# Unordered indirect writes and a different split of rounding work in an attention, mixture-of-experts and dense kernel

## The chip, the cores and the metric

The kernel runs on one core of a Trainium2 chip. The metric is the device time of one execution in microseconds (us); three runs of the kernel before are shown, and one further execution was profiled. A difference of under 1% is about what cannot be told from no change here.

## The reference

Three layers follow each other: attention whose queries are averaged in pairs, a mixture of eight experts of which each token takes one, and a dense layer with a squared ReLU. All data is float32.

```python
q_pool = q.reshape(B, H, S // 2, 2, D).mean(axis=3)
attn = softmax(q_pool @ k.T / sqrt(D))
x = (attn @ v) as (2304, 512)                  # B*S = 2304 tokens
expert_idx = argmax(normalized(x) @ normalized(emb).T / tau)
for e in range(8):                             # one expert for each token
    h = maximum(x[mask] @ w1[e], 0)            # 512 -> 1024
    out[mask] = gate_w[mask] * (h @ w2[e])     # 1024 -> 512
h = out @ w_in                                 # 512 -> 2048
g = maximum(h, 0) ** 2
result = g @ w_out                             # 2048 -> 512
```

## The kernel before

**Numbers as two halves.** TensorE multiplies 16-bit values. A float32 operand is kept as a high half (the value rounded by ScalarE, `hi`) and a low half (the value minus `hi`, by GpSimd or VectorE, `lo`), and each product is three matmuls: hi·hi, hi·lo, lo·hi. `w_in` and `w_out` lie in HBM as 64-bit numbers; `split64` first makes a float32 out of each pair of words with three VectorE operations (L1156, L1161, L1165), and then rounds it with ScalarE (L1170) and GpSimd (L1172). Such a unit of 128x512 is a *piece* here; each of the two matrices has 16 of them.

**Stages.** Attention and routing fill the first 500 us. The expert stage (some 500 to 757 us) goes over tiles of T = 192 rows sorted by expert. `tile_a(t)` multiplies by w1, ReLU goes to ScalarE (`hh`, L1281) and its low half to VectorE (`hl`, L1282), and `tile_b(t)` multiplies by w2. When the expert changes, `splits` makes the halves of the next expert's weights (`ws`): high halves by ScalarE and VectorE, low halves by VectorE and, for some, GpSimd (L1248). Into tiles 3 to 15 other work is dealt out: pieces of `w_in`, whose loads (`win_load`, L1149) GpSimd issues into two buffers of the tile `fill`; and, two for each of the tiles 3 to 11, the calls of `send`: an indirect DMA (L1132), also issued by GpSimd, that writes the gate and the row number of 128 tokens to their places in the HBM table `cm`. The rows are taken from `ci`, so that the program cannot know which rows of `cm` one write touches. SyncE loads weights (L1206) and transposed tokens (`x`, L1212).

**Dense layer.** `Ffn.run` takes the 2304 tokens in six blocks of 384. `first(tt)` computes 16 column groups `f` of the hidden layer (L1446, 12 matmuls each, called a *step* here); block 0 has its first 8 done in the expert stage (F1 = 8), so that `first(0)`, `first(1)`, `first(2)` are 40 steps, one after the other, before the first `second(tt)`. After a step's matmuls ScalarE takes the ReLU (L1451, `r`), VectorE squares it (L1452), and one step later `halves` makes `gh` by ScalarE (L1465) and `gl` by GpSimd (L1466). The steps' PSUM tiles come from two pools, chosen by `f % 5`: three buffers in `ps_b` and two in `ps_a`; `f` starts again at 0 in each block, so that f = 15, 0, 1, 2 follow each other in `ps_b`. During these 40 steps the generator `convert` also turns `w_out` into halves: after each step three parts of it are recorded.

**Order.** Every engine runs its instructions in the order in which this code records them. An engine waits on semaphores for data of others and for buffers to come free; the recording layer adds a wait for every earlier access to the same bytes.

Of the kernel before, what the change touches and what calls it, by code (L numbers as in the profile page):

```python
# [12 lines left out]
U32 = mybir.dt.uint32  # L13
ACTF = mybir.ActivationFunctionType
ALU = mybir.AluOpType
# [798 lines left out]
class Moe:  # L814
# [301 lines left out]
    def places(self, small):  # L1116

        nc = self.nc
        V = nc.vector
        d = small.tile([128, E], F32, tag="d", name="d")  # L1120
        V.tensor_tensor(out=d, in0=self.off[:, 1], in1=self.c("ecap"), op=ALU.subtract)
        pr = small.tile([128, 18, E], F32, tag="sq", name="prd")
        V.tensor_tensor(
            out=pr, in0=self.oh, in1=d[:, None, :].to_broadcast([128, 18, E]), op=ALU.mult
        )
        cp = small.tile([128, 18], F32, tag="cp", name="cp")
        V.tensor_reduce(out=cp, in_=pr, axis=AX.X, op=ALU.add)
        ci = small.tile([128, 18], I32, tag="ci", name="ci")
        V.tensor_tensor(out=ci, in0=cp, in1=self.rix, op=ALU.add)

        def send(n):
            nc.gpsimd.indirect_dma_start(  # L1132
                out=self.cm[:, :], out_offset=bass.IndirectOffsetOnAxis(ap=ci[:, n:n + 1], axis=0),
                in_=self.meta[:, n], in_offset=None, bounds_check=NTOK - 1,
            )

        return send

# [267 lines left out]
class Ffn:  # L1406
# [29 lines left out]
            self.hidden(0, f, ps, self.tmp[f % 2], self.g0[:, 0, f], self.g0[:, 1, f])  # L1436
            self.done += 1

    def hidden(self, tt, f, ps, r, gh, gl):
        nc = self.nc  # L1440
        c0 = slice(tt * self.N, tt * self.N + self.N)
        fs = slice(128 * f, 128 * f + 128)
        m = 0
        for k in range(4):
            for wh, yh in ((0, 0), (0, 1), (1, 0)):
                nc.tensor.matmul(  # L1446
                    out=ps, lhsT=half(self.win[wh][:, k, fs], wh), rhs=self.yT[yh][:, k, c0],
                    start=(m == 0), stop=(m == 11),
                )
                m += 1  # L1450
        nc.scalar.activation(out=r, in_=ps, func=ACTF.Relu)  # L1451
        nc.vector.scalar_tensor_tensor(  # L1452
            out=r, in0=ps, scalar=0.0, in1=r, op0=ALU.max, op1=ALU.mult
        )
        self.pend.append((r, gh, gl))
        if len(self.pend) > 1:
            self.halves()

# [2 lines left out]
            self.halves()  # L1461

    def halves(self):
        g, hi, lo = self.pend.pop(0)
        self.nc.scalar.activation(out=hi, in_=g, func=ACTF.Copy)  # L1465
        self.nc.gpsimd.tensor_tensor(out=lo, in0=g, in1=hi, op=ALU.subtract)  # L1466

    def run(self, ctx):
        nc, moe, N = self.nc, self.moe, self.N
        pool = lambda n, b, **kw: ctx.enter_context(moe.tc.tile_pool(name=n, bufs=b, **kw))  # L1470
        stg = pool("stg2", 2)
# [11 lines left out]
        so = {}  # L1483

        def wout_load(n):
            so[n] = stg.tile([128, 1024], U32, tag="g64", name="g64")
            moe.load64(so[n], moe.w_out[128 * n:128 * n + 128, :], nc.sync)

        def convert():
            for n in range(16):  # L1490
                f = stg.tile([128, 512], U32, tag="f32", name="f32")
                split = moe.split64(so.pop(n), f, wout[0][:, n], wout[1][:, n])
                for i, _ in enumerate(split):
                    yield
                    if i == 2:
                        yield
                if n + 2 < 16:
                    wout_load(n + 2)
                yield

        wout_load(0)
        wout_load(1)
# [5 lines left out]
        def first(tt):  # L1508
            g = G[tt] = {}
            for f in range(0 if tt else F1, 16):  # L1510
# [2 lines left out]
                gh, gl = [a[:, f % 8] for a in g[f // 8]]  # L1513
                ps = (ps_a if f % 5 in (3, 4) else ps_b).tile([128, N], F32, tag="a", name="a")
                r = rp.tile([128, N], F32, tag="r", name="r")
                self.hidden(tt, f, ps, r, gh, gl)
                if tt < 3:
                    for _ in range(3):
                        next(conv, None)
            self.finish()  # L1520

# [353 lines left out]
```

## Time and profile before

| | us |
|---|---|
| three runs | 1138.07, 1147.18, 1143.66 |
| median | 1143.66 |
| profiled execution, its own time | 1142.18 |
| span of its trace | 1140.4 |
| TensorE (PE) busy | 1061.1 (93%) |
| VectorE (DVE) busy | 722.1 (63%) |
| GpSimd (POOL) busy | 531.3 (47%) |
| ScalarE (ACT) busy | 527.5 (46%) |

TensorE is busy for nearly all of the span, so the rest of the reading is about the places where it is not, and about those where its granted clock is low. Times below count from the span's start.

### The profile page before, as it was taken

How to read it: one execution, taken by the hardware profiler on the slowest of the kernel's cores; microseconds unless marked ns; L12 is line 12 of the kernel's file. 1: busy time of each engine (PE TensorE's matmuls, PEld its weight loads, DVE VectorE, ACT ScalarE, POOL GpSimd, SP SyncE). 2: the span in 40 equal slices, each digit the busy share in tenths (PEclk: the TensorE clock that was granted, in tenths of full speed). 3: DMA queues.
4: the chain of work that ended last, by engine and by line, in shares of the span. 5: the costliest groups of instructions: out<-in, count | busy, mean ns of one | idle time of the engine just before them, and what ended most of it. 6: DMA issues, size and time to landing. Idle time of an engine off the chain costs nothing. (4 is left out here: it accounts for less than half of the span.)

```text
span 1140.4 us, 28256 instructions
## 1 busy us (share of the span) xinstructions
PE 1061.1 (93%) x11340; PEld 724.6 (64%) x11340; DVE 722.1 (63%) x1374; ACT 527.5 (46%) x998; POOL 531.3 (47%) x454
## 2 busy tenths in 40 slices
PE   6898899999999889999899799998799999999996
PEld 2465556656665566999899699975454454555543
DVE  6999989999998988866664548848850021211200
ACT  5776677678876756423222335534440031322200
POOL 4765655566765646522443426637760142322301
PEclk9999989999998989999999899999899999999998
DMA  8665765656766537569579699223310000000000
GB/s 221 146 141 155 192 160 123 145 141 143 155 135 139 110 67 194 142 190 226 103 96 231 140 228 272 55 52 104 108 38 19 29 10 20 10 10 20 10 19 28
DMA packets 170830, 128.98 MB, mean 113 GB/s; under 512 B 129816, under 2 KB 134040, under 8 KB 170672
## 3 DMA queue, kind: packets, MB, share of 16 engines
q1 hardware_dynamic: 164912, 109.09, 41.8%
q0 software_dynamic: 5760, 17.85, 5.2%
q8 instruction: 91, 1.49, 0.6%
q14 instruction: 67, 0.55, 0.2%
HBM read 74.69 MB, written 12.60 MB: 77 GB/s over the span
## 5 line engine op out<-in xcount | busy, mean ns | idle before, releaser
L425 POOL TENSOR_TENSOR pl<-p 128x512 f16<-128x512 f32 x144 | 176.8, 1233 | 155.1 <-ACT p L415 150.1
L415 ACT ACTIVATE p<-st 128x512 f32<-128x512 f32 x288 | 169.4, 598 | 81.1 <-PE st L397 78.2
L397 PE MATMUL st<-r,t 128*128 128x64 f16 (+3 forms) x1152 | 198.8, 294 | 8.3 <-ACT p L415 7.7
L1446 PE MATMUL a<-yT,win 128*128 128x384 f16 x1056 | 178.6, 333 | 11.3 <-DVE r L1452 8.8
L462 PEld LDWEIGHTS <-p 128*128 128x128 bf16 x2304 | 135.9, 99 | 59.6 <-issue 6.7
L1446 PEld LDWEIGHTS <-win 128*128 128x128 f16 (+1 forms) x1152 | 114.4, 99 | 89.7 <-issue 18.7
L462 PE MATMUL pv<-vx,p 128*128 128x65 f16 x2250 | 159.9, 197 | 2.4 <-DVE xb L503 2.4
L1531 PE MATMUL o<-wo,gh 128*128 128x512 f16 (+1 forms) x528 | 157.0, 379 | 0.0
L462 PE MATMUL pv<-vx,pl 128*128 128x65 f16 x1125 | 144.7, 194 | 0.0
L425 DVE TENSOR_TENSOR pl<-p 128x512 f16<-128x512 f32 x144 | 141.5, 984 | 3.5 <-ACT p L415 3.5
L1451 ACT ACTIVATE r<-a 128x384 f32<-128x384 f32 x88 | 42.6, 486 | 185.6 <-PE a L1446 138.6
L1398 PEld LDWEIGHTS <-ws 128*128 128x128 f16 (+1 forms) x1344 | 114.0, 100 | 15.7 <-POOLq L1218 9.5
L1538 DVE TENSOR_SCALAR ot<-o,cms 128x512 f32<-128x512 f32 x18 | 13.5, 750 | 171.4 <-PE o L1531 171.4
L1398 PE MATMUL fst<-hl,ws 128*128 128x192 f16 x448 | 112.0, 250 | 9.9 <-DVE hl L1282 9.9
L1398 PE MATMUL fst<-hh,ws 128*128 128x192 f16 x896 | 117.0, 250 | 3.3 <-POOLq L1218 3.3
L397 PEld LDWEIGHTS <-t 128*128 128x128 f16 (+1 forms) x1152 | 75.4, 99 | 69.8 <-issue 33.7
L367 DVE CUSTOM_DVE_ANT_0 rd<-sm,rd,mc 128x512 bf16<-128x512 f32 x144 | 106.2, 742 | 18.3 <-PE sm L341 6.5
L1466 POOL TENSOR_TENSOR gl<-r,gh 128x384 f16<-128x384 f32 x88 | 87.7, 1006 | 64.0 <-ACT gh L1465 63.8
L1386 PE MATMUL fsm<-x,ws 128*128 128x192 f16 x1344 | 113.2, 246 | 0.0
L1386 PEld LDWEIGHTS <-ws 128*128 128x128 f16 (+1 forms) x1344 | 111.1, 98 | 0.4
L462 PEld LDWEIGHTS <-pl 128*128 128x128 f16 x1152 | 111.1, 101 | 0.0
L1452 DVE SCALAR_TENSOR_TENSOR r<-a,r 128x384 f32<-128x384 f32 x88 | 48.9, 555 | 85.5 <-ACT r L1451 85.2
(250 smaller groups left out, 1727.2 us busy)
## 6 DMA issues: line engine op xcount, KB each, us to landing
stg<-in_moe_w SPq DMA_DIRECT2D x24, 1024.0 KB, 7.9
vr<-in_v SPq DMA_DIRECT2D x16, 576.0 KB, 4.5
kr<-in_k SPq DMA_DIRECT2D x15, 576.0 KB, 5.5
fill<-in_moe_w_in POOLq DMA_DIRECT2D x16, 512.0 KB, 7.4
g<-in_moe_w_out SPq DMA_DIRECT2D x16, 512.0 KB, 3.4
qr<-in_q SPq DMA_DIRECT2D x15, 512.0 KB, 5.3
t<-t SPq DMA_DIRECT2D x16, 288.0 KB, 3.8
xs<-tmp SPq DMA_DIRECT2D x16, 192.0 KB, 3.9
```

What stands on the lines that cost most here:

```text
L367: nc.vector.tensor_tensor_reduce(out=rd, in0=ps, in1=rd, scale=1.0, scalar=mc[:, slots:slots + 1], op0=ALU.add, op1=ALU.max, accum_out=mx[ ...
L397: nc.tensor.matmul(out=st[:, j * n:j * n + n], lhsT=lhs[0:kk, m, :], rhs=r[0:kk, c0:c0 + n], start=first, stop=(kk == 65), skip_group_chec ...
L415: nc.scalar.activation(out=p, in_=st[:, 0:p.shape[1]], func=ACTF.Exp, scale=SCALE)
L425: eng.tensor_tensor(out=pl, in0=s.pop(("p32", i)), in1=s["ph", i], op=ALU.subtract)
L462: nc.tensor.matmul(out=o[:, 0:vn], lhsT=s[p, i][:, cs:cs + w], rhs=vx[:, 9 * a_ + c, v0:v0 + vn], start=(u == 0 and p == "ph" and v0 == 0) ...
L1386: self.nc.tensor.matmul(out=ps[:, f, 0:w], lhsT=w1(wh, f2)[:, fs], rhs=x[:, 4 * xh + k, 0:w], start=(f == 0 and m == 0), stop=(m == 11), s ...
L1398: self.nc.tensor.matmul(out=yp[m // 2][:, m % 2, 0:w], lhsT=w2(wh, f)[:, ds], rhs=h(l, f), start=(f == i == m % 2 == 0), stop=(f == 7 and ...
L1446: nc.tensor.matmul(out=ps, lhsT=half(self.win[wh][:, k, fs], wh), rhs=self.yT[yh][:, k, c0], start=(m == 0), stop=(m == 11),)
L1451: nc.scalar.activation(out=r, in_=ps, func=ACTF.Relu)
L1452: nc.vector.scalar_tensor_tensor(out=r, in0=ps, scalar=0.0, in1=r, op0=ALU.max, op1=ALU.mult)
L1466: self.nc.gpsimd.tensor_tensor(out=lo, in0=g, in1=hi, op=ALU.subtract)
L1531: nc.tensor.matmul(out=ps, lhsT=at(l, f)[:, rs], rhs=half(wout[wh][:, f], wh), start=(m == 0), stop=(m == 47),)
```

## The change

There are three parts. The indirect writes of `send` are put in a group whose members need not wait for each other. In the dense layer's first three blocks (tt < 3) `gl` is made by VectorE, `eng=nc.vector`, in place of GpSimd. And `convert` is written anew: the rounding of piece n-1 (ScalarE, then GpSimd) is recorded between the VectorE operations of piece n, with 2 or 3 parts after a step in place of 3.

```diff
--- before.py
+++ after.py
@@ -1129,10 +1129,13 @@
         V.tensor_tensor(out=ci, in0=cp, in1=self.rix, op=ALU.add)
 
         def send(n):
-            nc.gpsimd.indirect_dma_start(
+            ins = nc.gpsimd.indirect_dma_start(
                 out=self.cm[:, :], out_offset=bass.IndirectOffsetOnAxis(ap=ci[:, n:n + 1], axis=0),
                 in_=self.meta[:, n], in_offset=None, bounds_check=NTOK - 1,
             )
+
+            self.tc.declare_no_dep(ins.ins, group="send", reason="rows apart")
+            self.tc.add_to_no_dep_group("send", ins.ins)
 
         return send
 
@@ -1436,7 +1439,7 @@
             self.hidden(0, f, ps, self.tmp[f % 2], self.g0[:, 0, f], self.g0[:, 1, f])
             self.done += 1
 
-    def hidden(self, tt, f, ps, r, gh, gl):
+    def hidden(self, tt, f, ps, r, gh, gl, eng=None):
         nc = self.nc
         c0 = slice(tt * self.N, tt * self.N + self.N)
         fs = slice(128 * f, 128 * f + 128)
@@ -1452,7 +1455,7 @@
         nc.vector.scalar_tensor_tensor(
             out=r, in0=ps, scalar=0.0, in1=r, op0=ALU.max, op1=ALU.mult
         )
-        self.pend.append((r, gh, gl))
+        self.pend.append((r, gh, gl, eng or nc.gpsimd))
         if len(self.pend) > 1:
             self.halves()
 
@@ -1461,9 +1464,9 @@
             self.halves()
 
     def halves(self):
-        g, hi, lo = self.pend.pop(0)
+        g, hi, lo, eng = self.pend.pop(0)
         self.nc.scalar.activation(out=hi, in_=g, func=ACTF.Copy)
-        self.nc.gpsimd.tensor_tensor(out=lo, in0=g, in1=hi, op=ALU.subtract)
+        eng.tensor_tensor(out=lo, in0=g, in1=hi, op=ALU.subtract)
 
     def run(self, ctx):
         nc, moe, N = self.nc, self.moe, self.N
@@ -1487,16 +1490,22 @@
             moe.load64(so[n], moe.w_out[128 * n:128 * n + 128, :], nc.sync)
 
         def convert():
-            for n in range(16):
-                f = stg.tile([128, 512], U32, tag="f32", name="f32")
-                split = moe.split64(so.pop(n), f, wout[0][:, n], wout[1][:, n])
-                for i, _ in enumerate(split):
+
+            late = iter(())
+            for n in range(17):
+                split = iter(())
+                if n < 16:
+                    f = stg.tile([128, 512], U32, tag="f32", name="f32")
+                    split = moe.split64(so.pop(n), f, wout[0][:, n], wout[1][:, n])
+                for i in range(3):
+                    next(split, None)
+                    if i == 2 and n + 2 < 16:
+                        wout_load(n + 2)
                     yield
-                    if i == 2:
+                    if i < 2:
+                        next(late, None)
                         yield
-                if n + 2 < 16:
-                    wout_load(n + 2)
-                yield
+                late = split
 
         wout_load(0)
         wout_load(1)
@@ -1513,9 +1522,9 @@
                 gh, gl = [a[:, f % 8] for a in g[f // 8]]
                 ps = (ps_a if f % 5 in (3, 4) else ps_b).tile([128, N], F32, tag="a", name="a")
                 r = rp.tile([128, N], F32, tag="r", name="r")
-                self.hidden(tt, f, ps, r, gh, gl)
+                self.hidden(tt, f, ps, r, gh, gl, nc.vector if tt < 3 else None)
                 if tt < 3:
-                    for _ in range(3):
+                    for _ in range(2 + f % 2):
                         next(conv, None)
             self.finish()
```

First place, GpSimd in the expert stage, tile 6: two sends, a load of `w_in`, branches around the weights' rounding. The brackets name the semaphores that an instruction waits for (DMASW: a DMA that GpSimd issued). Before:

```order
L1248 TENSOR_TENSOR ws<-stg_10965,ws 128x1024 [waits DMAHW3_49,DMAHW4_49,DMAHW2_49,DMAHW5_49,DMAHW1_49,DMAHW6_49,DMAHW0_49,DMAHW7_49,PE_49,Activation_49]
L1219 UNCONDITIONAL_BRANCH
L1218 UNCONDITIONAL_BRANCH [waits Pool_49]
L1172 TENSOR_TENSOR win_10912<-fill,win_10911 128x512 [waits Activation_49]
L1132 DMA cm<-meta,ci 2304x2 [waits DMASW0_49]
L1149 DMA fill<-in_moe_w_in 128x1024 [waits DMASW1_49,DVE_49]
L1132 DMA cm<-meta,ci 2304x2 [waits DMASW3_49]
```

The same place after:

```order
L1251 TENSOR_TENSOR ws<-stg_10965,ws 128x1024 [waits DMAHW3_49,DMAHW4_49,DMAHW2_49,DMAHW5_49,DMAHW1_49,DMAHW6_49,DMAHW0_49,DMAHW7_49,PE_49,Activation_49]
L1222 UNCONDITIONAL_BRANCH
L1221 UNCONDITIONAL_BRANCH [waits Pool_49]
L1175 TENSOR_TENSOR win_10912<-fill,win_10911 128x512 [waits Activation_49]
L1132 DMA cm<-meta,ci 2304x2
L1152 DMA fill<-in_moe_w_in 128x1024 [waits DMASW4_49,DMASW1_49,DVE_49]
L1132 DMA cm<-meta,ci 2304x2
```

Nothing moved; the two sends have lost their wait for the send before, and the load between them has one more wait, for an earlier user of its own semaphore. Nine of the 18 sends keep a wait of that kind.

Second place, VectorE in the dense layer, from the start of block 0 (r: the square; f: the three operations of a piece; gl: low half). Before:

```order
L1452 SCALAR_TENSOR_TENSOR r<-a,r 128x384 x2
L1156 TENSOR_SCALAR f_16720<-g_16656 128x512
L1161 SCALAR_TENSOR_TENSOR f_16720<-g_16656,f_16720 128x512
L1165 SCALAR_TENSOR_TENSOR f_16720<-g_16656,f_16720 128x512
L1452 SCALAR_TENSOR_TENSOR r<-a,r 128x384 x2
```

After:

```order
L1455 SCALAR_TENSOR_TENSOR r<-a,r 128x384
L1469 TENSOR_TENSOR gl<-r,gh 128x384
L1159 TENSOR_SCALAR f_16718<-g_16656 128x512
L1455 SCALAR_TENSOR_TENSOR r<-a,r 128x384
L1469 TENSOR_TENSOR gl<-r,gh 128x384
L1164 SCALAR_TENSOR_TENSOR f_16718<-g_16656,f_16718 128x512
L1168 SCALAR_TENSOR_TENSOR f_16718<-g_16656,f_16718 128x512
```

Two low halves have come in for each piece, and the three operations of a piece now stand in two groups, one after the first and two after the second of two steps.

Third place, ScalarE at the same point (wo: the high half of a piece of `w_out`). Before:

```order
L1451 ACTIVATE r<-a 128x384 x2
L1465 ACTIVATE gh<-r 128x384
L1170 ACTIVATE wo_16648<-f_16676 128x512
L1451 ACTIVATE r<-a 128x384
L1465 ACTIVATE gh<-r 128x384
L1451 ACTIVATE r<-a 128x384
L1465 ACTIVATE gh<-r 128x384
L1170 ACTIVATE wo_16648<-f_16720 128x512
```

After:

```order
L1454 ACTIVATE r<-a 128x384 x2
L1468 ACTIVATE gh<-r 128x384
L1454 ACTIVATE r<-a 128x384
L1468 ACTIVATE gh<-r 128x384
L1173 ACTIVATE wo_16648<-f_16676 128x512
L1454 ACTIVATE r<-a 128x384
L1468 ACTIVATE gh<-r 128x384
L1454 ACTIVATE r<-a 128x384
```

The rounding of a piece stands one step later, behind the ReLU of the step after the piece's last VectorE operation.

## Rows read from the trace of the kernel before

**Rows 1.** The chain that ended last: start us, us, what.

```profile
765.10 1.16 DVE f L1156
...
913.76 31.20 PE a L1446 x192
```

**Rows 2.** Windows: length, PE, PEld, DVE, ACT, POOL busy us (count), PEclk, DMA, GB/s.

```profile
630.00:640.00 10.00, 4.59 (x33) 4.09 (x33) 4.32 (x7) 3.39 (x4) 3.31 (x3) 0.66 0.65 51
640.00:650.00 10.00, 10.00 (x125) 10.00 (x123) 9.93 (x11) 6.20 (x10) 5.01 (x2) 1.00 0.62 211
650.00:660.00 10.00, 8.05 (x78) 7.66 (x77) 1.49 (x3) 0.00 (x0) 4.09 (x3) 0.83 0.58 143
```

**Rows 3.** Timeline, TensorE, expert stage: start us, us, instruction, idle before and its releaser.

```profile
634.81 0.32 PE L1398 MATMUL fst<-hl,ws 128*128 128x192 f16 x1 [5.30 <-DVE hl L1282]
635.72 0.50 PE L1398 MATMUL fst<-hh,ws 128*128 128x192 f16 x2 [0.60 <-POOLq L1218]
655.32 0.34 PE L1398 MATMUL fst<-hh,ws 128*128 128x192 f16 x2 [1.95 <-POOLq L1218]
```

**Rows 4.** Timeline, VectorE, there.

```profile
612.49 0.69 DVE L1165 SCALAR_TENSOR_TENSOR fill<-fill 128x512 uint32<-128x512 uint32 x1
...
633.86 0.43 DVE L1156 TENSOR_SCALAR fill<-fill 128x512 uint32<-128x512 uint32 x1 [7.46 <-DMA fill<-in_moe_w_in]
634.21 0.55 DVE L1282 SCALAR_TENSOR_TENSOR hl<-fsm,hh 128x384 f16<-128x384 f32 x1
```

**Rows 5.** Timeline, GpSimd, there.

```profile
612.74 1.34 POOL L1132 DMA_INDIRECT cm<-meta,ci  x1 [6.54 <-DMA cm<-meta,ci]
...
616.00 0.59 POOL L1149 DMA_DIRECT2D fill<-in_moe_w_in  x1
...
635.20 1.04 POOL L1132 DMA_INDIRECT cm<-meta,ci  x1 [14.33 <-DMA cm<-meta,ci]
...
651.92 0.98 POOL L1132 DMA_INDIRECT cm<-meta,ci  x1 [6.49 <-DMA cm<-meta,ci]
653.15 2.11 POOL L1248 TENSOR_TENSOR ws<-stg,ws 128x1024 bf16<-128x1024 f32 x1 [0.25 <-issue]
```

**Rows 6.** Timeline, TensorE, the dense layer's first 40 steps.

```profile
758.24 21.34 PE L1446 MATMUL a<-yT,win 128*128 128x384 f16 x120 [2.49 <-PEq L1373]
782.68 29.04 PE L1446 MATMUL a<-yT,win 128*128 128x384 f16 x168 [3.10 <-DVE r L1452]
...
821.52 30.08 PE L1446 MATMUL a<-yT,win 128*128 128x384 f16 x168 [5.57 <-DVE r L1452]
```

**Rows 7.** Timeline, VectorE, ScalarE and GpSimd, one piece of w_out there.

```profile
788.33 0.56 DVE L1452 SCALAR_TENSOR_TENSOR r<-a,r 128x384 f32<-128x384 f32 x1 [0.61 <-ACT r L1451]
...
788.80 0.63 DVE L1156 TENSOR_SCALAR f<-g 128x512 uint32<-128x512 uint32 x1
...
789.11 2.42 POOL L1466 TENSOR_TENSOR gl<-r,gh 128x384 f16<-128x384 f32 x2
789.47 1.28 DVE L1161 SCALAR_TENSOR_TENSOR f<-g,f 128x512 uint32<-128x512 uint32 x1
790.79 1.29 DVE L1165 SCALAR_TENSOR_TENSOR f<-g,f 128x512 uint32<-128x512 uint32 x1
...
792.11 0.63 ACT L1170 ACTIVATE wo<-f 128x512 f16<-128x512 f32 x1 [2.61 <-DVE f L1165]
...
792.82 1.16 POOL L1172 TENSOR_TENSOR wo<-f,wo 128x512 bf16<-128x512 f32 x1 [1.29 <-ACT wo L1170]
...
793.15 0.56 DVE L1452 SCALAR_TENSOR_TENSOR r<-a,r 128x384 f32<-128x384 f32 x1 [0.61 <-ACT r L1451]
```

**Rows 8.** One line's instructions: engine, operation, count, ns min/median/max, first and last start.

```profile
L425 DVE TENSOR_TENSOR plx<-p32x x1: 550/550/550, 445.8 to 445.8; 128x384 f16<-128x384 f32 x1
...
L1161 DVE SCALAR_TENSOR_TENSOR f<-g,f x16: 694/1284/1291, 766.3 to 838.0; 128x512 uint32<-128x512 uint32 x16
...
L1156 DVE TENSOR_SCALAR fill<-fill x16: 416/586/2347, 520.2 to 633.9; 128x512 uint32<-128x512 uint32 x16
```

## Prediction

> **What bounds the kernel now.** I read the chain of waits first. It ends in matmuls, and of the dense layer it says two things: from 913.76 us 192 matmuls of 384 columns take 31.20 us, which is 16 steps of 1.95 us at the full rate, and that from 765.10, a piece's first operation, the chain runs through VectorE's work [rows 1] until TensorE starts again at 821.52 [rows 6]. The windows come next, to find where a TensorE that is busy 93% of the time is not at work. Attention and routing hold nothing that is changed, so only two places are left. In the expert stage, windows of 10 us hold 125 matmuls when nothing is wrong, and 33 and 78 in two of them, where the granted clock is also low [rows 2]. In the dense layer's first 40 steps TensorE stands still for 3.10 and 5.57 us [rows 6]. Then I read, at each place, who released the waiting engine.
>
> Expert stage, about 635 us: TensorE waited 5.30 us for the low half `hl` and then 0.60 us for GpSimd to get past a branch [rows 3]. VectorE, which makes `hl`, stood before it in L1156, 7.46 us for a load of `w_in` [rows 4]. GpSimd issued that load at 616.00; its buffer had been free from 612.49 + 0.69 = 613.18, but GpSimd had sat until 612.74 before a send that waited 6.54 us for the send before, and had work to make up [rows 4, 5]. The branch came late because of the next send, which waited 14.33 us and started at 635.20 [rows 5]. About 655 us: TensorE waited 1.95 us for GpSimd, whose weight rounding L1248 (2.11 us, from 653.15) stood behind a send that had waited 6.49 us [rows 3, 5].
>
> Dense layer: VectorE needs 793.15 - 788.33 = 4.82 us for a piece of `w_out` and two steps, TensorE 2 x 1.95 = 3.90 [rows 1, 7]. TensorE runs ahead as far as PSUM lets it, and where a block ends four steps in a row use the three buffers of `ps_b`; there it waits for the square of the step three before. Those are the two stalls.
>
> **The change part by part.** The sum is made against the profiled execution, 1142.18 us (span 1140.4 and 1.8 around it), which lies 1.5 below the median 1143.66 and within the three runs.
>
> *Sends.* What is at stake is the idle time and the low clock that follows it. At 635 us: 5.30 + 0.60 idle. The window's 33 matmuls took 4.59 us in which 4.59 x 12.5 = 57 go at full rate; 24 lost x 0.08 us = 1.9. Together 7.8. At 655 us: 1.95 idle, and 8.05 x 12.5 = 101 against 78, 23 x 0.08 = 1.8; together 3.75 [rows 2, 3]. The waits of the sends go. Nine of 18 keep a wait on a semaphore, but for a DMA eight issues back, which by then has landed unless it takes longer than anything in these rows. So GpSimd issues the last load at about 613.2, when its buffer is free, in place of 616.0, and the one before earlier too. Needed is it when TensorE came to stand, 634.81 - 5.30 = 629.5: the load took 633.86 - 616.00 = 17.9 us, so even at that length it lands at 631.1 and returns 2.8 of the 5.30; if it also lands faster because the load before it is through by then, all. The branch wait and the L1248 wait go fully, since both follow a send on GpSimd's queue. Bounds: 2.8 + 0.6 + 3.75 = 7.1 and 11.55; nothing if the load comes no earlier, then 4.35. I take 11, near the upper end: the low clock goes with the stall that caused it. Other engines' work at the same time is unchanged, so I set nothing against it here; the price of GpSimd working earlier is a rival below. In the other tiles with sends TensorE loses little to GpSimd, and I count nothing.
>
> *Low halves on VectorE.* Per piece, from start to start: a square costs 0.47 (788.33 to 788.80), two 0.94 [rows 7]. A low half of 128x384 from SBUF has one row, 0.55 us alone [rows 8]; with the overlap that the square shows (0.56 against 0.47) 0.47, two 0.94. L1156 alone is 0.42 [rows 8]. L1161 alone is 0.69, L1165 the same [rows 8]; with 0.02 between them and 0.08 of overlap at the end 1.32. Sum 3.62, below TensorE's 3.90. Out of the 4.82 go the 0.61 that VectorE waited for ScalarE's ReLU, which stood behind the rounding of the piece just made (L1170, 2.61 us idle before it) [rows 7], since that rounding now comes a step later; and the stretch of L1161 and L1165 beside GpSimd's two low halves: 1.28 and 1.29 in place of 0.69 [rows 7, 8].
>
> What stays on GpSimd is L1172, 1.16 us a piece [rows 7]. ScalarE's rounding now follows `gh`, and L1172 follows that, so it starts about when VectorE goes from a square to a low half and L1156: beside operations that the rows show to be slowed. One low half on GpSimd cost VectorE 1.28 - 0.69 = 0.59 us [rows 7, 8]; the lower bound for L1172 is that, the upper its whole length, 1.16. A piece then takes 4.21 to 4.78 us, and I take the middle, 4.50.
>
> The Trainium skill, page "SBUF — State Buffer", section "Who interferes with whom", says that a VectorE instruction with two SBUF inputs and a GpSimd instruction that reads SBUF exclude each other: whichever is first holds the shared port pair to its end. By that rule L1172 can cost VectorE its whole 1.16 us, which is the upper bound: 4.78 a piece. It speaks against this part of the change, because the low halves that came over to VectorE have two SBUF inputs; the pair of 2.42 us beside 1.28 and 1.29 [rows 7] agrees with operations that take turns.
>
> From VectorE's first operation on a piece (765.10) to the release of the second stall (821.52) lie 56.4 us [rows 1, 6], 11.7 pieces of 4.82. At 4.50 each that point comes 11.7 x 0.32 = 3.7 us earlier, and with it the end of the 40 steps, since the last 168 matmuls follow without a wait [rows 6]. TensorE would be there at about 758.2 + 1.8 (its first ten steps took 21.34 for 19.5) + 26 x 1.95 = 810.7 [rows 6], so VectorE still sets it. Bounds: 0.5 (4.78) and 7.1 (4.21). The 8 steps after the last piece have no such work, and VectorE's 0.94 a step fits into 1.95: nothing. ScalarE's work is the same in amount.
>
> *Sum*: 1142.2 - 11 - 3.7 = 1127.5; I say 1128, as the profiled execution lies a little under the median.
>
> **The rivals.**
> The load lands no earlier, because other transfers hold it up as before: for it speaks that it took 17.9 us; against it, that the load in front of it goes out earlier too. The stall of 5.30 and its 1.9 stay: 1142.2 - 4.35 - 3.7 = 1134.1.
> VectorE is not in the way at all: L1172 falls beside squares, which read PSUM and kept 0.54 to 0.56 us beside it [rows 7], and a piece takes 3.62. TensorE sets the pace: the 40 steps end at 758.2 + 1.8 + 78 = 838.0 in place of 821.52 + 30.08 = 851.6, 13.6 less: 1117.6.
> L1172 costs its whole length in each piece, as operations of the two engines take turns: a piece of 4.78, 1142.2 - 11 - 0.5 = 1130.7. This is what the Trainium skill's page, named above, would give.
> Slower: the sends' waits kept GpSimd's weight rounding (L1248) away from VectorE's, and without them the two meet, so that `hl` is late by up to 2.11 us [rows 5] and TensorE falls to the low clock as at 655, 1.8 more: 3.9 for each. One, two or three leave a gain; from four on the 14.7 are gone, and with five it is 1142.2 - 14.7 + 19.5 = 1147. Against it: there are few such roundings in the stretch of the sends, and two of them are the ones that came too late.
> The change doesn't do what it says: the waits that nine sends keep hold GpSimd as before. Then only the dense part is left, 1138.5; against it, eight issues lie between.
>
> **How the numbers follow.** Forecast 0.44 (1128, itself 1123 to 1133); late load 0.18; TensorE's pace 0.14; whole length 0.14; slower 0.05; no effect of the sends 0.05. The range 1116 to 1137 leaves out the last two. A measurement of this kernel can tell about 1%, 11.4 us, from no change, so faster means below 1132.2: nearly all of the forecast (0.41), TensorE's pace (0.14), two thirds of the whole length (0.09), a third of the late load (0.06), 0.70. Slower than 1155.1: 0.03. The rest, 0.27, within.
>
> **What would show it.** On GpSimd no send with an idle time of several microseconds for the send before it; windows at 630 to 660 with some 125 matmuls and full clock; L1156 without a wait of 7 us. In the dense layer a period of VectorE of about 4.5 us a piece, L1161 and L1165 near 0.69, the time lost in L1156 or the low half instead; the first TensorE stall gone, the second still there; the 40 steps ending some 3.7 us sooner after their start. The prediction is wrong if TensorE waits for `hl` at new places, if the load of `w_in` still lands after 629 us, or if the period is under 4.2 or over 4.8.

## The result and the profile after

The changed kernel took 1130.27 us (median of four, 1126.43 to 1132.83) beside 1142.72 for the kernel before in the same session: a ratio of 0.9896, 95% interval 0.985 to 0.9942. A second session gave 1130.23 (twelve runs) and the same ratio, 0.9855 to 0.9938. That is 11.9 us faster (1142.7 x 0.0104); forecast were 14.7 against the profiled execution, 1128 us. Here and below a ratio and its interval leave out runs more than 1.5% above the fastest of the same kernel, a median keeps them; where the two say different things, the text goes by the ratio. Both executions of the first comparison that have a trace lie near their medians: 1142.18 and 1131.79 us, spans 1140.4 and 1130.0.

To compare traces in which attention took a few microseconds more or less, I cut each at two marks: the start of the matmul that makes the routing table (the last piece of routing) and the first matmul of the dense layer's 40 steps. Between the marks lies the expert stage. It took 264.12 us before (494.12 to 758.24) and 259.45 after (495.32 to 754.77): 4.7 less. The stretch from the first mark to the first matmul of the first expert tile has the same work in both traces and lies ahead of all that was changed, but it ran at another clock. As windows (length, busy us and counts of PE, PEld, DVE, ACT, POOL, then granted clock, DMA share, GB/s), before and after:

```profile
494.12:500.32 6.20, 6.20 (x75) 6.20 (x76) 1.32 (x4) 1.17 (x3) 0.00 (x0) 1.00 0.60 144
495.32:503.17 7.85, 7.85 (x75) 7.69 (x76) 1.32 (x4) 1.17 (x3) 0.00 (x0) 0.78 0.64 172
```

These 1.65 us are not the change's doing: another execution of the changed kernel took 6.19 there. Counted from the first tile the stage took 257.92 before and 251.60 after, 6.3 less.

The 40 steps took 93.36 before (758.24 to 821.52 + 30.08) and 86.47 after (754.77 to 812.10 + 29.14): 6.9 less. Everything else is within 1.2 us.

The timeline of TensorE in the dense layer after, to be read against [rows 6]: start, length, instruction, and in brackets the idle time and its releaser.

```profile
754.77 52.80 PE L1449 MATMUL a<-yT,win 128*128 128x384 f16 x312 [2.32 <-PEq L1376]
812.10 29.14 PE L1449 MATMUL a<-yT,win 128*128 128x384 f16 x168 [4.52 <-DVE r L1455]
```

The first stall (3.10) is gone, 312 matmuls run through; the second is there, 1.05 shorter, and the matmuls behind it take 29.14 in place of 30.08.

One piece of `w_out` after, on VectorE, then GpSimd's rows beside it; it answers to [rows 7].

```profile
782.78 0.55 DVE L1469 TENSOR_TENSOR gl<-r,gh 128x384 f16<-128x384 f32 x1
783.24 1.39 DVE L1159 TENSOR_SCALAR f<-g 128x512 uint32<-128x512 uint32 x1
784.55 0.55 DVE L1455 SCALAR_TENSOR_TENSOR r<-a,r 128x384 f32<-128x384 f32 x1
785.02 0.54 DVE L1469 TENSOR_TENSOR gl<-r,gh 128x384 f16<-128x384 f32 x1
785.49 0.68 DVE L1164 SCALAR_TENSOR_TENSOR f<-g,f 128x512 uint32<-128x512 uint32 x1
786.20 0.69 DVE L1168 SCALAR_TENSOR_TENSOR f<-g,f 128x512 uint32<-128x512 uint32 x1
786.81 0.55 DVE L1455 SCALAR_TENSOR_TENSOR r<-a,r 128x384 f32<-128x384 f32 x1
787.27 0.55 DVE L1469 TENSOR_TENSOR gl<-r,gh 128x384 f16<-128x384 f32 x1
787.74 1.38 DVE L1159 TENSOR_SCALAR f<-g 128x512 uint32<-128x512 uint32 x1
```

```profile
783.13 1.21 POOL L1175 TENSOR_TENSOR wo<-f,wo 128x512 bf16<-128x512 f32 x1 [3.28 <-ACT wo L1173]
787.63 1.21 POOL L1175 TENSOR_TENSOR wo<-f,wo 128x512 bf16<-128x512 f32 x1 [3.29 <-ACT wo L1173]
```

The piece takes 787.74 - 783.24 = 4.50. L1164 and L1168 are at their 0.69 and the wait for ScalarE is gone; what is left over TensorE's 3.90 stands in one row, L1159, which starts 0.11 us after GpSimd's low half and takes 1.39 in place of 0.43: it ends 0.29 us after GpSimd's (784.63 and 784.34).

The same windows as [rows 2], after, and ahead of them one more:

```profile
540.00:550.00 10.00, 7.63 (x74) 7.31 (x71) 8.50 (x10) 2.71 (x5) 5.53 (x4) 0.83 0.64 107
...
630.00:640.00 10.00, 6.47 (x78) 6.10 (x76) 5.82 (x9) 4.92 (x7) 2.42 (x2) 1.00 0.38 42
640.00:650.00 10.00, 6.62 (x79) 6.24 (x78) 9.96 (x9) 4.33 (x7) 8.63 (x5) 1.00 0.66 213
650.00:660.00 10.00, 10.00 (x124) 10.00 (x122) 3.19 (x6) 1.32 (x3) 1.75 (x2) 1.00 0.95 223
```

From 630 to 660 us the clock stays full, but 78 and 79 matmuls in place of 125 say that TensorE still stands. Its timeline there, to be read against [rows 3]; at its head an earlier place, where the kernel before had three waits for `hl` (1.75, 2.20 and 0.60 us, from 541.91 to 551.23):

```profile
545.38 0.24 PE L1401 MATMUL fst<-hl,ws 128*128 128x192 f16 x1 [2.37 <-DVE hl L1285]
...
633.27 0.24 PE L1401 MATMUL fst<-hl,ws 128*128 128x192 f16 x1 [2.92 <-DVE hl L1285]
...
649.65 0.24 PE L1401 MATMUL fst<-hl,ws 128*128 128x192 f16 x1 [2.58 <-DVE hl L1285]
```

All waits for GpSimd are gone (0.73, 0.60 and 1.95 us before), and these three wait for `hl`. (Two more, of 0.61 and 0.81 us at 638.09 and 643.02, are for weights that VectorE was still rounding; the kernel before had none of that kind.) Why TensorE waits for `hl` is in VectorE's rows (against [rows 4]) and then in GpSimd's (against [rows 5]):

```profile
632.33 0.43 DVE L1159 TENSOR_SCALAR fill<-fill 128x512 uint32<-128x512 uint32 x1 [6.05 <-DMA fill<-in_moe_w_in]
632.67 0.55 DVE L1285 SCALAR_TENSOR_TENSOR hl<-fsm,hh 128x384 f16<-128x384 f32 x1
...
645.67 3.46 DVE L1251 TENSOR_TENSOR ws<-stg,ws 128x1024 bf16<-128x1024 f32 x1
649.06 1.01 DVE L1285 SCALAR_TENSOR_TENSOR hl<-fsm,hh 128x384 f16<-128x384 f32 x2
```

```profile
614.76 0.57 POOL L1152 DMA_DIRECT2D fill<-in_moe_w_in  x1 [2.39 <-DVEq L1221]
...
620.40 1.06 POOL L1132 DMA_INDIRECT cm<-meta,ci  x1 [0.16 <-issue]
621.76 1.01 POOL L1132 DMA_INDIRECT cm<-meta,ci  x1 [0.30 <-issue]
...
642.04 1.78 POOL L1132 DMA_INDIRECT cm<-meta,ci  x1 [0.16 <-issue]
644.13 1.75 POOL L1132 DMA_INDIRECT cm<-meta,ci  x1 [0.30 <-issue]
645.92 2.12 POOL L1251 TENSOR_TENSOR ws<-stg,ws 128x1024 bf16<-128x1024 f32 x1
```

The sends stand back to back: their idle times of 6.5 and 14.3 us are gone. But the load that GpSimd now issues at 614.76 is used at 632.33, 17.6 us later, almost as late as before; and GpSimd, no longer behind a send, makes its low half of a weight piece (2.12) beside VectorE's, which takes 3.46 instead of 1.22. So at 650 us a wait of 2.58 for `hl` stands where TensorE had waited 1.95 for GpSimd. At 545 us it is the same: L1251 took 3.50 from 541.37, beside GpSimd's from 541.61, and there the low clock followed the wait: 74 matmuls and a granted clock of 0.83 in the window from 540 to 550.

### The profile page after: what moved, and what is told of

Read it like the earlier page. It is cut to its first block, busy times and chain, and to the rows that moved or that the text cites. A ratio compares the mean times of both kernels' runs of the same rounds, so it can differ in the third digit from the quotient of the medians.

```text
span 1130.0 us, 28225 instructions
## 1 busy us (share of the span) xinstructions
PE 1053.7 (93%) x11297; PEld 723.6 (64%) x11340; DVE 732.4 (65%) x1414; ACT 529.3 (47%) x998; POOL 490.0 (43%) x414
## 5 line engine op out<-in xcount | busy, mean ns | idle before, releaser
L1449 PE MATMUL a<-yT,win 128*128 128x384 f16 x1056 | 175.9, 330 | 7.0 <-DVE r L1455 4.5
L1540 PE MATMUL o<-wo,gh 128*128 128x512 f16 (+1 forms) x513 | 153.8, 379 | 0.0
L364 ACT ACTIVATE rd<-sm 128x512 bf16<-128x512 f32 x144 | 85.9, 599 | 35.9 <-PE sm L341 32.5
L1540 PE MATMUL o<-wo,gl 128*128 128x512 f16 x264 | 100.1, 379 | 0.8
```

What stands on the lines that cost most here:

```text
L364: nc.scalar.activation(out=s["rd"], in_=ps, func=ACTF.Relu)
L1449: nc.tensor.matmul(out=ps, lhsT=half(self.win[wh][:, k, fs], wh), rhs=self.yT[yh][:, k, c0], start=(m == 0), stop=(m == 11),)
L1540: nc.tensor.matmul(out=ps, lhsT=at(l, f)[:, rs], rhs=half(wout[wh][:, f], wh), start=(m == 0), stop=(m == 47),)
```

## The experiments

Two questions were open. In the dense layer: is it taking turns with GpSimd that makes VectorE's piece long (theory: each low half on GpSimd costs VectorE nearly its own length), or the order and amount of VectorE's own work (rival)? In the expert stage, which gave 4.7 us where 11 were forecast: is it the landing of the last load (theory), or GpSimd's work that meets VectorE's (rival), or were the sends' waits worth little (rival)?

### Each part alone

The sends alone, or the dense layer's two edits alone, on the kernel before:

```
-            nc.gpsimd.indirect_dma_start(
+            ins = nc.gpsimd.indirect_dma_start(
...
+            self.tc.declare_no_dep(ins.ins, group="send", reason="rows apart")
+            self.tc.add_to_no_dep_group("send", ins.ins)
```

> Only the sends are declared free; the dense layer is that of before. My theory, from the two traces: from the table's matmul to the dense layer's first matmul the change took 264.1 to 259.4 us, so this kernel is 4 to 5 us faster than before (about 1138), its dense 40 steps take 93.4 us as before, and TensorE still waits for hl near 545, 633 and 650 us, where VectorE's weight rounding (L1248 there, one of 3.4 us or more) meets GpSimd's. Rival, the forecast on record: 11 us faster (1131 to 1132), with no such waits.

> Only the dense layer is changed; the sends wait for each other as before. My theory: the 40 steps take 86.5 us as in the changed kernel, so the kernel is 6.9 us faster than before (about 1136), and the 5.3 us wait near 635 us is back, with the half clock. Rival, the forecast on record: 3.7 us faster (1139). A second rival, that the two parts need each other: the two gains fall short of the whole by more than 3 us.

Measured over twelve runs each, beside 1140.9 for the kernel before: sends alone 1134.35, ratio 0.9942 (0.9898 to 0.9986), 6.6 us faster by the ratio; dense alone 1131.3, ratio 0.9941 (0.9896 to 0.9985), 6.7 us faster by the ratio (9.6 by the medians). Each interval reaches from under 2 to nearly 12 us, so the times say that each part is a gain; that the two share it about evenly and add up fits them, but they don't show it closely. In the traces the 40 steps took 92.8 us with the old dense code and 86.6 with the new, as in the pair above (93.36 and 86.47). The expert stage took 261.77 with the sends free and 261.21 without: this trace of the sends shows hardly anything, though the times do. TensorE's waits near 545, 633 and 650 us were there with the sends alone, as the theory said; the wait of 5.3 us that I expected back with the dense part alone was 2.32.

### The dense layer's two edits apart

On the kernel before, first the low halves `gl` on VectorE alone (old order of the rounding), then the later rounding alone (`gl` on GpSimd):

```
-                self.hidden(tt, f, ps, r, gh, gl)
+                self.hidden(tt, f, ps, r, gh, gl, nc.vector if tt < 3 else None)
```

> On the kernel before: gl by VectorE in the first three blocks, but w_out's rounding where it was. Theory A, that the two engines exclude each other while both read SBUF, and that what counts is beside what GpSimd's L1172 falls: here it starts with a low half and holds up the next one for about half of its length, so a piece takes about 4.1 to 4.3 us, less than the 4.49 of the changed kernel, and the 40 steps 82 to 84 us. Theory B, that ScalarE's ReLU behind the rounding was what VectorE waited for: the 0.61 us wait stays, a piece takes 4.6 or more, the 40 steps 88 to 91 us.

> On the kernel before: w_out's rounding one piece later, but gl by GpSimd. Theory A: a piece takes about 4.5 us, since the wait of 0.61 for ScalarE goes and the two low halves on GpSimd still stretch VectorE's operations; the 40 steps take 86 to 88 us. Theory C, that the low halves on VectorE bring the whole gain: the piece stays at 4.8 us and the 40 steps at 93 us.

With `gl` on VectorE alone a piece took 4.16 us and the 40 steps 84.4 (762.93 to 818.19 + 29.14), less than in the changed kernel; with the later rounding alone 4.56 and 87.3 (755.92 to 814.08 + 29.14). Both lie at the theory's numbers (84.4 is 0.4 over the 82 to 84 it gave) and far from the rival's. The 0.61 us wait for ScalarE, which the rival kept, is gone in the first run too, where the rounding stands as before. (These two runs and the next were made once each: 1137.88, 1133.78 and 1122.58 us. Single times say nothing in this scatter; only their traces are used.) VectorE's rows of a piece in the first of the two, then GpSimd's low half beside them:

```profile
793.10 0.55 DVE L1466 TENSOR_TENSOR gl<-r,gh 128x384 f16<-128x384 f32 x1
793.79 0.56 DVE L1452 SCALAR_TENSOR_TENSOR r<-a,r 128x384 f32<-128x384 f32 x1
794.26 0.81 DVE L1466 TENSOR_TENSOR gl<-r,gh 128x384 f16<-128x384 f32 x1
795.00 0.41 DVE L1156 TENSOR_SCALAR f<-g 128x512 uint32<-128x512 uint32 x1
```

```profile
793.46 1.21 POOL L1172 TENSOR_TENSOR wo<-f,wo 128x512 bf16<-128x512 f32 x1 [2.95 <-ACT wo L1170]
```

GpSimd's 1.21 us begin while VectorE is at a low half and then a square, which reads PSUM and keeps its 0.56; only the last 0.4 us fall on an operation that is held, 0.81 in place of 0.55. In the changed kernel the same 1.21 us begin just ahead of L1159 and cost it 0.95. So each edit alone is a gain, and the later rounding costs 0.3 us a piece once `gl` is on VectorE.

### The transposed loads

The two loads of activations that share the DMA engines with the last load of `w_in` are left out:

```
-            if t >= TMAX:
+            if t >= TMAX or t in (11, 12):
```

> The changed kernel without the two transposed loads of activations (x from xs) that are issued at about 611 and 626 us, those of the expert tiles 11 and 12; these two tiles compute with activations of earlier tiles. In the changed kernel the last load of w_in was issued at 614.76 and VectorE waited for it until 632.33, 17.6 us later, while the DMA engines were busy the whole time but moved only 40 to 150 GB/s from 618 on. Theory A, the transposes hold the load up: without them it lands within 5 to 9 us (the queue's other loads of 512 KB took 3.6 to 8), by 620 to 624, VectorE's L1159 starts in time, and the wait of TensorE at about 633 us (2.92 us for hl) is gone; the expert stage, from the routing table's last matmul to the dense layer's first, takes 256 to 257.5 us in place of 259.5. Theory B, the four weight loads of 1 MB issued at 597.8 to 609.6 hold it up, or the sends do: it lands 15 to 18 us after its issue as before, and the wait of 2 to 3 us stays.

The stage took 249.84 us, 6 to 8 less than theory A had said, and VectorE didn't wait for a load. But the next two runs, which have these transposes, took 249.09 and 250.93 and had the load in 10.2 and 10.9 us. So the stage is some ten microseconds shorter where the load isn't late; whether the transposes make it late stays open.

### Two low halves moved to VectorE

In the expert stage the low half of piece 6 of an early expert's weights; in the dense layer that of `w_out`:

```
-POOL_LO = (3, 6)
+POOL_LO = (3,)
```

```
-                    split = moe.split64(so.pop(n), f, wout[0][:, n], wout[1][:, n])
+                    split = moe.split64(so.pop(n), f, wout[0][:, n], wout[1][:, n], nc.vector)
```

> The changed kernel, and of the eight pieces in which an early expert's weights are split, the low half of piece 6 by VectorE in place of GpSimd (piece 3 stays). In the changed kernel the two stood beside each other twice, and VectorE's own low half of 1024 columns (L1251) took 3.50 and 3.46 us in place of 1.22, after which TensorE waited 2.37 and 2.58 us for hl. Theory A, the sends' freedom lets GpSimd's low half meet VectorE's and the two exclude each other: both of VectorE's low halves take 1.2 us each, 2.4 together where 3.5 went, the two waits for hl shrink by about 1.1 us each, and the expert stage takes 256 to 258.5 us (259.45 and 261.77 with the sends free so far); the time is 1 to 3 us under the changed kernel's. Theory B, hl is late because VectorE has too much work there, whoever it meets: with 1.2 us more of work on VectorE for each change of expert the waits stay or grow, stage 259.5 to 263, the time as the changed kernel's or up to 3 us more.

> The changed kernel, and the low halves of w_out (L1175, 1.21 us a piece on GpSimd) by VectorE too, so that GpSimd has no work left in the first 40 steps of the dense layer. Theory A, GpSimd's 1.21 us cost VectorE nearly their whole length (L1159 1.38 beside them, 0.43 alone): the piece on VectorE is 3.62, as measured in the first piece, plus one low half of 512 columns at about 0.6, 4.1 to 4.3 us in place of 4.49; the 40 steps take 79 to 83 us in place of 86.5, the time is 4 to 7 us under the changed kernel's 1130.3, ratio to the kernel before about 0.984. Theory B, VectorE is the bound by its own work and GpSimd's work beside it costs less than its length: the piece takes 4.9 to 5.1, the 40 steps 92 to 96, the time 5 to 9 us over the changed kernel's, ratio about 0.997.

Piece 6: 1126.15 us, ratio 0.9889 (0.9846 to 0.9932); the times show no difference from the changed kernel's 0.9896. In the trace VectorE's two low halves took 1.22 each where one had taken 3.5, and TensorE's waits for `hl` were 0.6 us in all, the stage 249.09 (the theory gave 256 to 258.5; the load was in time as well); the wait at 545 us is 0.35. In the other traces with free sends and piece 6 on GpSimd the longest wait there was 1.1 to 3.9 us. With held sends the waits at that place came to as much (4.55 in the profiled execution before, 3.7 with the dense part alone); 2.80 of the 4.55 and 2.34 of the 3.7 stand behind a low half that GpSimd made late. So the meeting is real and in part takes the place of an older wait; what is gained without it is too small for these times.

`w_out`: 1121.9 us, ratio 0.9827 (0.9783 to 0.987), beyond the changed kernel's 0.9896, though the ends of the two intervals (0.985 to 0.9942 there) overlap. TensorE's timeline of the 40 steps, then one piece on VectorE:

```profile
748.72 2.60 PE L1449 MATMUL a<-yT,win 128*128 128x384 f16 x15 [2.50 <-PEq L1376]
751.96 75.85 PE L1449 MATMUL a<-yT,win 128*128 128x384 f16 x465 [0.64 <-issue]
```

```profile
767.35 0.42 DVE L1159 TENSOR_SCALAR f<-g 128x512 uint32<-128x512 uint32 x1
767.69 0.55 DVE L1455 SCALAR_TENSOR_TENSOR r<-a,r 128x384 f32<-128x384 f32 x1
768.15 0.55 DVE L1469 TENSOR_TENSOR gl<-r,gh 128x384 f16<-128x384 f32 x1
768.62 0.68 DVE L1164 SCALAR_TENSOR_TENSOR f<-g,f 128x512 uint32<-128x512 uint32 x1
769.22 0.68 DVE L1175 TENSOR_TENSOR wo<-f,wo 128x512 bf16<-128x512 f32 x1
769.83 0.68 DVE L1168 SCALAR_TENSOR_TENSOR f<-g,f 128x512 uint32<-128x512 uint32 x1
770.43 0.55 DVE L1469 TENSOR_TENSOR gl<-r,gh 128x384 f16<-128x384 f32 x1
770.90 0.55 DVE L1455 SCALAR_TENSOR_TENSOR r<-a,r 128x384 f32<-128x384 f32 x1
771.36 0.41 DVE L1159 TENSOR_SCALAR f<-g 128x512 uint32<-128x512 uint32 x1
```

With one operation more VectorE's piece is shorter: 771.36 - 767.35 = 4.01, and the 40 steps take 79.1 us with no wait for VectorE. The operation costs 0.61 on VectorE (769.22 to 769.83); on GpSimd it cost VectorE 0.95 (1.38 less 0.43 for L1159). That settles the dense layer: the bound was VectorE's own work plus what GpSimd took from it.

### The last load

The changed kernel again, then the changed kernel and the kernel before without the last load of `w_in` (its piece is made from what the buffer held):

```
-            if n < 16:
+            if n < 15:
```

> The changed kernel, unaltered, for a second trace and more times beside the runs below. The expert stage (from the routing table's last matmul to the dense layer's first) has taken 259.45 and 261.77 us where the last load of w_in landed 141 to 149 us after that matmul's start counted the same way and VectorE waited 6 us for it, and 249.1 to 250.9 where it landed by 126 to 128. Theory A, the landing of that one load decides: the stage is either 249 to 253, without a wait of VectorE for the load, or 258 to 262, with one of 5 us or more. Theory B, the stage depends on something else of the execution: it lies between, or a short stage comes with a long wait for the load. Median 1125 to 1131.

> The changed kernel without the last of the sixteen loads of w_in; its piece is made from what the buffer held, with the same instructions on every engine, so the dense layer's result is wrong in 512 columns of one quarter. Theory A, the late landing of this load is what a stage of 259 to 262 us has over one of 250: the stage takes 249 to 253 us, no wait of VectorE of over 3 us for a load of w_in, no half clock between 625 and 660 us; the time is steadier and 3 to 8 us under the unaltered changed kernel's median of the same runs. Theory B, the stage is long for another reason (weights of the experts that land late, GpSimd beside VectorE): 256 to 262, and the time as the unaltered kernel's within 2 us.

> The kernel before, sends still waiting for each other, without the last of the sixteen loads of w_in (its piece made from what the buffer held, as in the run above). Theory A, held sends cost by making this load late: the waits for hl and the low clock at about 635 us are gone and the stage takes 253 to 258 us in place of 261.2 to 264.1; what stays are the waits for GpSimd (2 to 4 us with their low clock). The time is 5 to 10 us under the kernel before's. Theory B, held sends cost mainly through GpSimd's own late work, not through the load: the stage takes 259 to 263, the time 0 to 3 us under the kernel before's.

(In the first of these texts "141 to 149" is a slip: 632.33 - 495.32 = 137 us in the changed kernel and 139 with the sends alone.) The unaltered changed kernel gave another picture this time, a run of 1116.97 us with a stage of 252.29. GpSimd's row and VectorE's:

```profile
607.23 0.57 POOL L1152 DMA_DIRECT2D fill<-in_moe_w_in  x1 [2.39 <-DVEq L1221]
```

```profile
618.11 0.43 DVE L1159 TENSOR_SCALAR fill<-fill 128x512 uint32<-128x512 uint32 x1 [1.45 <-DMA fill<-in_moe_w_in]
```

The load was there in 10.9 us in place of 17.6, 130 us after the routing table's matmul in place of 137, and the stage is 7.2 us shorter, 5.5 counted from the first tile. GpSimd's low halves met VectorE's here as well (3.49 and 3.48 us), but where VectorE wasn't late from the load TensorE waited only 0.74 us behind the second of them. With the load left out the stage took 251.21 and the times 1122.46 (1118.14 to 1128.28, six runs), beside 1130.23 (1116.97 to 1138.70, twelve) unaltered. The ratios are 0.985 (0.9798 to 0.9903) and 0.9896 (0.9855 to 0.9938); they overlap, and of the nine unaltered runs in the ratio five lie above the highest of the six. So where the sends are free the traces fit theory A, and the times lean to it without showing it.

Where the sends are held, theory B's numbers came: without the last load the kernel before took 1139.66 us, ratio 1.0006 (0.9965 to 1.0047), and its stage 261.51. GpSimd's row of the load that is then the last, and TensorE's waits there:

```profile
622.25 1.03 POOL L1132 DMA_INDIRECT cm<-meta,ci  x1 [6.04 <-DMA cm<-meta,ci]
623.82 0.58 POOL L1149 DMA_DIRECT2D fill<-in_moe_w_in  x1 [0.53 <-issue]
```

```profile
636.21 0.24 PE L1398 MATMUL fst<-hl,ws 128*128 128x192 f16 x1 [1.15 <-DVE hl L1282]
648.21 5.95 PE L1386 MATMUL fsm<-x,ws 128*128 128x192 f16 x70 [1.61 <-DVE ws L1248]
658.75 0.34 PE L1398 MATMUL fst<-hh,ws 128*128 128x192 f16 x2 [0.46 <-POOLq L1218]
...
695.76 0.34 PE L1398 MATMUL fst<-hh,ws 128*128 128x192 f16 x2 [3.27 <-POOL ws L1248]
```

A send now holds up the load before the last instead, and TensorE waited 5.9 us for GpSimd in the stage, 3.27 of it at 695.76. So the single load isn't all that held sends cost; here they cost at other work of GpSimd's that was due.

All traces beside each other (us; "from tile 0" is the stage without the stretch at its start that took 6.2 us in some executions and 7.85 in others; "load" is when VectorE used the last load, counted from the routing table's matmul; "for GpSimd" and "for hl" are TensorE's waits in the stage; its waits for weights that VectorE rounds, at most 1.6 us, are left out):

```
kernel                     stage   from tile 0   load   for GpSimd   for hl   40 steps
sends held
  before                   264.12    257.92     139.7     3.3        9.9      93.4
  dense alone              261.21    255.01     135.1     5.7        4.0      86.6
  gl on VectorE alone      263.38    257.19     136.3     5.8        5.7      84.4
  later rounding alone     263.11    256.91     137.3     4.3        7.7      87.3
  before, last load out    261.51    255.31       -       5.9        2.3      93.0
sends free
  changed                  259.45    251.60     137.0     0          7.9      86.5
  sends alone              261.77    255.58     139.0     0          9.2      92.8
  changed, again           252.29    246.10     130.0     0          4.7      86.1
  piece 6 on VectorE       249.09    241.25     126.5     0          0.6      85.3
  w_out on VectorE         250.93    243.09     128.3     0          2.3      79.1
  both                     248.89    242.70     128.4     0          1.3      78.8
  two transposes out       249.84    241.99     127.2     0          1.4      86.0
  last load out            251.21    245.02       -       0          3.6      86.3
```

### Both together

> The changed kernel with the two edits that made it faster together: the low halves of w_out and of piece 6 of an early expert's weights by VectorE. In the runs of each alone the 40 steps took 79.1 us (86.5 in the changed kernel) and TensorE's waits for hl 0.6 us. Theory A, the two lie in different stages and add up: 40 steps in 79 to 80 us, stage 249 to 252 where the load lands in time, median 1116 to 1122, ratio to the kernel before 0.978 to 0.983. Theory B, the gain at piece 6 is scatter of the executions and adds nothing: median 1120 to 1125 as with w_out's low halves alone, ratio 0.981 to 0.986, waits for hl of 2 us or more again.

1117.9 us (1110.81 to 1127.69), ratio 0.982 (0.9758 to 0.9882): faster than the kernel before, by its middle value faster than the changed kernel, and as far as these times tell the same as with `w_out` alone. In the trace both effects stand, 78.8 us and waits for `hl` of 1.3. The median lies in theory A's range alone, the ratio in both, so which of the two is right is not decided; by the traces and the times of each alone `w_out`'s low halves carry most of the gain.

## Why the prediction was right

**The sum.** 14.7 us forecast, 11.9 measured, inside the range. Two terms were off in opposite ways: the sends gave less, by 4 to 6 us, the dense layer more, by 3. That the sum came this close is partly luck. Two of the signs of being wrong that the prediction names came as well: VectorE used the last load at 632.33, after 629, and TensorE waited for `hl` at a new place, 649.65. Its windows with 125 matmuls at 630 to 650 did not come.

**The dense layer: mechanism right, size too small.** A piece was forecast at 4.50 us and measured 4.43 to 4.50 from the second on, L1161 and L1165 (now L1164 and L1168) are at 0.69, the first stall is gone and the second stayed. The mis-sized term is the 3.7 us: measured 6.9, by traces 93.36 to 86.47, and 6.7 with this part alone. It counted only the regular piece. From VectorE's first operation on a piece to its twelfth piece it gained 52.64 - 48.41 = 4.23: 0.61 of that is the first piece, which had no GpSimd beside it and took 3.54 (4.15 before). The square that ends the second stall now stands behind one operation of the piece, not three: 1.90 from the piece's start to TensorE's in place of 3.78, 1.9 more. And the matmuls behind it lost less to the low clock: 0.9. With 0.2 lost at the start these make 6.9. One reason given was not needed: the 0.61 us for ScalarE's ReLU was to go because the rounding comes a step later, but it went with the low halves on VectorE alone; VectorE then had work (793.10 to 793.65 in those rows) while ScalarE caught up, and 0.14 us were left.

**L1172's price.** Taken was the middle of 0.59 and 1.16; it cost 0.95. The rival of its whole length (4.78 a piece) was nearer in mechanism than in time: operations that take turns, but GpSimd's 1.21 us begin while VectorE's low half in front (782.78, 0.55 as when alone) is still running, so that L1159 is held only for the rest. The Trainium skill, page "SBUF — State Buffer", section "Who interferes with whom", has VectorE and GpSimd exclude each other for the whole of an instruction where both use the port pair that they share. In the rows shown the traces agree with it (2.12 beside 3.46 in place of 1.22). TensorE's pace, a rival at 0.14, didn't come, but the run with `w_out` on VectorE came within 0.11 us a piece of it.

**The sends: the step that failed is "I take 11, near the upper end".** With the sends alone the times gave 6.6 us (1.6 to 11.6), and 5 by the difference between the changed kernel and the dense part alone (0.9896 against 0.9941). The trace of the changed kernel gave 4.7, or 6.3 counted from the first tile. The GpSimd waits did go, as said, in every trace with free sends. The rest hung on the load, and there both ends of the bounds came, roughly. Counted from the first tile, the four full traces with held sends took 255 to 258 us. With free sends the two in which the load came late took 251.6 and 255.6: 1 to 5 less than the 257 in the middle of the held ones, which is the rival of the late load (4.35). Two with the same code in the expert stage and the load in time took 246.1 and 243.1: 11 and 14 less. (Two more in time had piece 6 moved as well.) And the stall of 5.30 us with its low clock, from which most of the 11 was taken, was the worst of its kind: in the other three full traces with held sends the longest wait for `hl` was 2.3 to 2.7.

**"I set nothing against it here" failed too.** The slower rival's meeting of weight roundings exists: low halves of 3.50 and 3.46 us in place of 1.22, and TensorE waits of 2.37 and 2.58 us. It came twice, not four times, and at both places where GpSimd's lateness had cost something before. In place of the 1.95 us and the low clock at 655 that the sum counted as gone, a wait of 2.58 us for `hl` came at the full clock; at 545 the low clock came too. What a meeting costs hangs on the load again: where it was in time, low halves of the same 3.48 us left TensorE waiting 0.74 and 0.75 us in place of 2.58.

**Open** is why the same load, from issue to use, takes 10 to 12 us in four executions with free sends and 17.6 to 17.8 in two.

## What to carry to other kernels

Work that is moved from a busy VectorE to GpSimd pays where it falls beside VectorE operations that read PSUM, and may not elsewhere: the same low half cost VectorE 0.95 us in the changed kernel, about 0.26 where most of it fell beside a square, and 0.61 when VectorE made it. Write down for each operation on GpSimd what it costs its neighbour, and move it back where that exceeds what VectorE would need itself. A stall read from one execution is one draw: where a transfer's landing decides it, price the removal at both ends and give the chance to each, and don't take one trace's worst wait as what there is to gain. When a false wait is taken away from a queue, look at what the freed engine will now run beside.

## What the runs showed of the hardware that I had not expected

A TENSOR_SCALAR with a single SBUF input, L1159, is held by GpSimd as the two-input operations are: 0.43 us alone, 1.32 to 1.39 beside a low half of 1.16 to 1.21. I had priced it from two-input rows.

Issuing an indirect write took GpSimd about 1.0 us (1.01 to 1.06 in the rows after), and 1.75 to 1.78 where VectorE was at its weight roundings (642.04 and 644.13 us there).

The same program took 1116.97 to 1138.70 us in twelve runs, with a mean granted clock of 0.980 in the fastest and 0.959 in the slowest. The load's landing is only part of that. Of the 14.8 us between the two traces of the changed kernel (spans 1130.0 and 1115.2) 7.2 lie in the expert stage and 7.3 ahead of it, in attention and routing (first mark at 495.32 and 488.07), where nothing was changed; what makes those differ is not shown here.

A wait of TensorE for `hl` was followed by the low clock in some places and not in others: the 2.37 us at 545 in the changed kernel were (0.83 and 74 matmuls in the window from 540 to 550 us), the 2.92 and 2.58 us at 633 and 650 were not.
